# GpSimd computes nothing in the first expert slot: all low parts go to VectorE, and six weight pieces are decoded through PSUM

## The chip, the cores and the metric

One core of one Trainium2 chip runs the whole program. The metric is device time in microseconds (us). The engines are TensorE (PE; PEld is its weight load), VectorE (DVE), ScalarE (ACT), GpSimd (POOL) and SyncE (SP, which only issues DMAs here).

## The reference: what is computed

Three stages follow each other, all in float32 with 3072 tokens of width 384.

```python
# 1. linear attention with a decay: per batch, head and step t
y[t]  = r[t] @ (state + outer(u * k[t], v[t]))
state = w[t][:, None] * state + outer(k[t], v[t])
# 2. mixture of 8 experts, 384 tokens each, filled greedily by score
logits = x @ w_gate                  # tokens taken in order of their logits
out[mask_e] = relu(x[mask_e] @ w1[e]) @ w2[e]
# 3. a dense block, its weights w_in and w_out given as float64
h = x @ w_in
y = (h * clip(h + 3, 0, 6) / 6) @ w_out
```

## The kernel before

**Stages.** Attention runs first, as 24 iterations `n` (blocks of 128 tokens), in `attention`. Then `search` and `fill` find the 384 tokens of the first expert while nothing else can run on TensorE; `gather` fetches their rows by three indirect DMAs that GpSimd issues (line 958). Then come eight expert slots, `slot(p, ...)`. A slot has eight steps `f` of the expert's own layers (products `ph` and `pa`; "up part" below), and then 16 steps of the dense block (products `pg` and `py`, steps 0 to 17 with the drain; "dense part"). Search, fill and gather for expert p + 1 are cut into pieces by `yield` and run inside slot p.

**High and low parts.** Every float32 operand of a big product is split into a high part (rounded to `fp32r` by ScalarE) and a low part (value minus high part), and each product takes three of the four partial products. The low parts are `wl` (expert weights, 128x768, line 933), `hl` (hidden values, lines 995 and 998), `gl` (dense block, line 1021), `xl` (inputs, lines 969 and 1049) and the second half of `io` (dense weights, line 897).

**Decoding.** The dense block's weights come as 32 pieces of 128x384 float64, loaded into `raw`. A piece is turned into float32 by: `Abs` on ScalarE (`q`, line 862), a clamp (line 865 on GpSimd or 875 on VectorE), and three integer operations on VectorE (lines 879, 881, 883: shift, sign, lowest bits). ScalarE then makes its high part and line 897 its low part. All pieces are decoded once, and serve the eight slots. In attention 12 pieces (`EARLY`) are decoded, with the intermediate `z` in PSUM (tag `cnt`), their clamps and ten of their low parts on GpSimd. Pieces 12 to 19 are clamped by GpSimd too, at the end of attention and in the search, and one operation of line 879 stands behind each of the search's six steps (`begin`). The rest, in pairs and in SBUF (`io_stages`), is spread over slot 0: `FIRST` stages behind the gather, and then `STAGES[half]` stages in each half step.

**Order.** Nothing is scheduled by the compiler; each engine executes in the order in which the program issues. In a slot, `dve()` opens each half step: it runs what is due (`run_due`: the high and low parts of decoded pieces), then in slot 0 the decode stages, then one piece of the search if its countdown `state["wait"]` is zero. `pe()` counts down and issues the search's small matmuls. `WAITS` holds the countdowns of slot 0. `tick(t)` issues loads and the expert weights' splits.

```python
1020  nc.scalar.activation(gh, g, AF.Copy)
1021  (nc.vector if last and f >= NGT - 2 else nc.gpsimd).tensor_tensor(gl, g, gh, op=ALU.subtract)
```

These stand right behind lines 1016 (ScalarE, `r`) and 1017 (VectorE, `r`); the matmuls that read `gl(f)` are issued two steps later (`down2(f - 2)`).

Of the kernel before, what the change touches and what calls it, by code (L numbers as in the profile page):

```python
# [9 lines left out]
F32 = mybir.dt.float32  # L10
# [32 lines left out]
FIRST = 4  # L43
SATW = 2
KHDVE = (23,)
HLPOOL = (3, 6)
SPLIT0 = 22
LODVE = (0, 1)
ABSAT = 1
SPLIT = 21  # L50
QB = 8
EARLY = 12
LATER = (14, 42)
PACK = 4
STAGES = (2, 1, 0, 2, 0, 2, 3, 0, 1, 1, 2, 0, 1, 1, 3, 0, 1, 0, 0, 3, 0, 1, 0, 3, 0, 2, 0, 1, 2, 1, 1, 2, 0, 1, 1, 0, 0, 0, 0, 2, 0, 0, 0, 0, 0, 0, 0, 0)
WAITS = (2, 1, 3, 2, 2, 2, 2, 2, 2, 2, 3, 2, 2, 4, 2, 2, 2, 2, 2, 1)
# [3 lines left out]
B0 = 7  # L60
# [9 lines left out]
class Kernel:  # L70
    def __init__(self, tc, ctx, t, out):
# [7 lines left out]
        self.begun, self.q, self.raw, self.io, self.io_at = {}, {}, {}, {}, 0  # L79
# [68 lines left out]
    def attention(self):  # L148
        tc, nc, t = self.tc, self.nc, self.t
        with ExitStack() as ctx:  # L150
# [236 lines left out]
            turn = {B0 + i * 4 // 3: i for i in range(EARLY)}  # L387
            bits, his, los = iter(()), [], []

            for n in range(NU + 2):  # L390
# [6 lines left out]
                for i in range(EARLY):  # L397
                    if n == B0 + i * 4 // 3 - 3:
                        self.io_load(i)
# [236 lines left out]
    def search(self, ph, mk, es, ve):  # L636

        nc, RT, ps_r = self.nc, self.RT, self.ps_r
# [19 lines left out]
        for k, (sh, n) in enumerate(steps):  # L658
            sh2, n2 = steps[k + 1] if k + 1 < len(steps) else (0, 0)

            if ph or k:
# [33 lines left out]
            if not ph:  # L695
                self.begin(EARLY + k)
            yield SATW
            pn = ps_r.tile([128, E], F32, tag="rt", name=f"pn{ph}_{k}")
# [41 lines left out]
    def fill(self, ph):  # L740
        nc, RT, ps_r = self.nc, self.RT, self.ps_r
# [19 lines left out]
        pb = ps_r.tile([128, 2], F32, tag="rt", name=f"pb{ph}")  # L761
# [18 lines left out]
        pl = ps_r.tile([32 * pack, 24 * pack], F32, tag="rt", name=f"pl{ph}")  # L780
# [12 lines left out]
        else:  # L793
# [4 lines left out]
            times(nc.vector, OBP, NU)  # L798
        yield 3
# [10 lines left out]
        py = ps_r.tile([128, 24], F32, tag="rt", name=f"py{ph}")  # L810
# [27 lines left out]
        pc = ps_r.tile([128, E, NU], F32, tag="rt", name=f"pc{ph}")  # L838
# [29 lines left out]
    def io_bits(self, i):  # L868

        nc = self.nc  # L870
        v = self.raw[i].rearrange("p (n t) -> p n t", t=2)
        low, top, q = v[:, :, 0], v[:, :, 1], self.q[i]
        qi = q.bitcast(I32)
# [4 lines left out]
        z = self.ps_c.tile([128, DM], I32, tag="cnt", name=f"z{i}") if i < EARLY else qi  # L878
        nc.vector.tensor_scalar(z, qi, 3, 0x3FFFFFF8, op0=ALU.logical_shift_left, op1=ALU.bitwise_and)
        yield  # L880
        nc.vector.scalar_tensor_tensor(z, top, -0x40000000, z, op0=ALU.bitwise_and, op1=ALU.bitwise_or)  # L881
        yield
        nc.vector.scalar_tensor_tensor(qi, low, 29, z, op0=ALU.logical_shift_right, op1=ALU.bitwise_or)  # L883

    def begin(self, i):
        b = self.begun.setdefault(i, [self.io_bits(i), 0])
        next(b[0], None)
        b[1] += 1
# [5 lines left out]
    def io_lo(self, i):  # L894
        w = self.io[i]
        eng = self.nc.vector if i in LODVE else self.nc.gpsimd
        eng.tensor_tensor(w[:, DM:], self.q.pop(i), w[:, 0:DM], op=ALU.subtract)  # L897

    def io_stages(self):

        while self.io_at < 2 * NGT:
            j = self.io_at
            self.io_at += 2
            for k in range(3 if j in self.clamped else 4):
                some = False
                for i in (j, j + 1):
                    if i not in self.begun or self.begun[i][1] <= k:
                        self.begin(i)
                        some = True
                if k == ABSAT:  # L910
                    while j + 3 - QB in self.q:
                        self.run_due()
                    for i in (j + 2, j + 3):
                        if i not in self.clamped:
                            self.io_abs(i)
                if some:
                    yield
            self.later(1, lambda j=j: (self.io_hi(j), self.io_hi(j + 1)))
            self.later(2, lambda j=j: (self.io_lo(j), self.io_lo(j + 1)))

# [10 lines left out]
    def split(self, raw, hi, lo, eng):  # L931
        self.nc.scalar.activation(hi, raw, AF.Copy)  # L932
        eng.tensor_tensor(lo, raw, hi, op=ALU.subtract)  # L933

# [36 lines left out]
    def slot(self, p, dve, pe, tick):  # L971
# [16 lines left out]
        def up_ev(f, ph):  # L988
            hh = self.HB.tile([128, CAP], F32R, tag="hh", name=f"hh{p}_{f}", bufs=2)
            hl = self.HB.tile([128, CAP], F32R, tag="hl", name=f"hl{p}_{f}", bufs=2)  # L990
            if p == 0 and f in HLPOOL:
                h = self.HB.tile([128, CAP], F32, tag="r6", name=f"h{p}_{f}", bufs=2)
                nc.scalar.activation(h, ph, AF.Relu)
                nc.scalar.activation(hh, h, AF.Copy)
                nc.gpsimd.tensor_tensor(hl, h, hh, op=ALU.subtract)
            else:
                nc.scalar.activation(hh, ph, AF.Relu)  # L997
                nc.vector.scalar_tensor_tensor(hl, ph, 0.0, hh, op0=ALU.max, op1=ALU.subtract)  # L998
# [292 lines left out]
```

## Time and profile before

| | us |
|---|---|
| three timed runs | 899.45 (898.15 to 905.95) |
| the profiled execution | 900.43 |
| its span, first to last instruction | 898.6 |
| busy: PE, DVE, ACT, POOL | 844.7, 523.4, 426.6, 464.1 |
| first product of slot 0, of slot 1, of slot 2 | 229.53, 333.50, 414.55 |

The profile is one execution; all positions are us from the start of its span. A busy PE in attention includes matmuls on constants that fill gaps. The share of the whole span says little: PE is busy 94% of it, but the losses lie in one stretch, between the end of attention (about 193 us) and slot 1.

### The profile page before, as it was taken

The page shows a single profiled execution, that of the slowest core. Times are in us where ns is not written, and L with a number is a line of the kernel's source. Part 1 is how long each engine was busy: PE and PEld are TensorE (multiplying, and loading weights), DVE is VectorE, ACT ScalarE, POOL GpSimd, SP SyncE. Part 2 cuts the span into 40 slices and gives each one's busy share as a digit, 9 for nine tenths or more (in the row PEclk, how much of TensorE's full clock was granted, in tenths as well). Part 3 has the DMA queues.
Part 4 walks back from the last instruction along what each step waited for, and adds up shares of the span by engine and source line. Part 5 has one row for each costly group of instructions (what it writes and reads, how often), then busy time and mean ns, then how long its engine had stood idle before and what let it go on. Part 6 is the DMA issues. An engine that isn't in the chain of part 4 may idle for free.

```text
span 898.6 us, 15952 instructions
## 1 busy us (share of the span) xinstructions
PE 844.7 (94%) x5942; PEld 790.1 (88%) x5942; DVE 523.4 (58%) x1269; ACT 426.6 (47%) x1025; POOL 464.1 (52%) x428
## 2 busy tenths in 40 slices
PE   7999999964669999999999999999999999999996
PEld 4889998852568899999999999999999999999996
DVE  6879998847798765654563655355455622422211
ACT  4777777731445453444344443434444353344332
POOL 4558898744673553346337423723662383365232
PEclk7999999975779999999999999999999999999999
DMA  9997777124610050023004101300320130122000
GB/s 251 255 262 224 214 220 225 48 62 173 200 47 1 1 168 27 1 89 106 1 3 132 61 1 54 123 19 1 110 85 1 53 114 27 54 62 80 1 1 27
DMA packets 40343, 80.48 MB, mean 90 GB/s; under 512 B 4416, under 2 KB 20160, under 8 KB 40256
## 3 DMA queue, kind: packets, MB, share of 16 engines
q1 hardware_dynamic: 32576, 62.06, 23.2%
q0 software_dynamic: 3072, 9.44, 3.2%
q10 hardware_dynamic: 4608, 7.87, 2.5%
q8 instruction: 49, 0.80, 0.4%
q14 instruction: 38, 0.31, 0.1%
HBM read 69.91 MB, written 9.44 MB: 88 GB/s over the span
## 4 chain that ended last, share of the span: by engine, by line
PE 62%; DVE 7%; issue 4%; POOL 2%; ACT 1%; DMA 0%; POOLq 0%; ACTq 0%; DVEq 0%
PE pg L980 20%; PE ph L980 10%; PE py L1031 7%; PE py L1029 6%; PE py L1030 6%; PE pa L1004 3%; PE pa L1006 3%; PE pa L1005 3%; POOL gl L1021 1%; DVE q L883 1%; DVE cm L669 1%; PE cnt L679 1%; PE px L966 1%; DVE q L881 1%; POOL io L897 1%
## 5 line engine op out<-in xcount | busy, mean ns | idle before, releaser
L1021 POOL TENSOR_TENSOR gl<-r,gh 128x384 fp32r<-128x384 f32 x126 | 131.9, 1047 | 263.7 <-ACT gh L1020 263.4
L980 PE MATMUL pg<-xh,io 128*128 128x384 f32 x768 | 160.5, 344 | 0.0
L1017 DVE SCALAR_TENSOR_TENSOR r<-r,pg 128x384 f32<-128x384 f32 x128 | 70.6, 552 | 139.7 <-ACT r L1016 138.3
L933 POOL TENSOR_TENSOR wl<-we,wh 128x768 fp32r<-128x768 f32 x60 | 115.4, 1925 | 57.4 <-ACT wh L932 38.4
L980 PEld LDWEIGHTS pg<-xh,io 128*128 128x128 f32 x768 | 131.8, 188 | 2.2 <-ACT xh L1048 1.6
L1031 PE MATMUL py<-io,gl 128*128 128x384 f32 x384 | 130.7, 340 | 1.7 <-POOL gl L1021 1.6
L1029 PE MATMUL py<-io,gh 128*128 128x384 f32 x384 | 131.3, 342 | 0.0
L1030 PE MATMUL py<-io,gh 128*128 128x384 f32 x384 | 129.0, 336 | 0.0
L1016 ACT ACTIVATE r<-pg,three 128x384 f32<-128x384 f32 x128 | 74.3, 580 | 110.0 <-PE pg L980 108.3
L1020 ACT ACTIVATE gh<-r 128x384 fp32r<-128x384 f32 x128 | 67.2, 525 | 104.1 <-DVE r L1017 104.1
L980 PE MATMUL pg<-xl,io 128*128 128x384 f32 x384 | 87.6, 336 | 0.0
L1031 PEld LDWEIGHTS py<-io,gl 128*128 128x128 f32 x384 | 72.0, 188 | 5.2 <-POOL gl L1021 4.9
L998 DVE SCALAR_TENSOR_TENSOR hl<-ph,hh 128x384 fp32r<-128x384 f32 x62 | 34.4, 555 | 71.8 <-ACT hh L997 71.8
L932 ACT ACTIVATE wh<-we 128x768 fp32r<-128x768 f32 x64 | 53.6, 838 | 40.0 <-PE pa L1006 22.6
L1029 PEld LDWEIGHTS py<-io,gh 128*128 128x128 f32 x384 | 72.2, 188 | 0.2
L1030 PEld LDWEIGHTS py<-io,gh 128*128 128x128 f32 x384 | 72.2, 188 | 0.0
L980 PEld LDWEIGHTS pg<-xl,io 128*128 128x128 f32 x384 | 68.7, 188 | 0.0
L980 PE MATMUL ph<-xh,wh 128*128 128x384 f32 x192 | 67.6, 352 | 0.1
L1006 PE MATMUL pa<-hl,wh 128*128 128x384 f32 x192 | 65.4, 341 | 1.4 <-DVE hl L998 0.7
L1004 PE MATMUL pa<-hh,wh 128*128 128x384 f32 x192 | 66.3, 346 | 0.0
L980 PE MATMUL ph<-xh,wl 128*128 128x384 f32 x192 | 65.8, 343 | 0.0
L1005 PE MATMUL pa<-hh,wl 128*128 128x384 f32 x192 | 65.0, 338 | 0.0
(221 smaller groups left out, 1690.7 us busy)
## 6 DMA issues: line engine op xcount, KB each, us to landing
we<-in_w SPq DMA_DIRECT2D x64, 384.0 KB, 3.1
kr<-in_kr SPq DMA_DIRECT2D x24, 448.0 KB, 6.2
raw<-in_wio SPq DMA_DIRECT2D x24, 384.0 KB, 5.4
w<-in_wp SPq DMA_DIRECT2D x24, 226.2 KB, 6.3
v<-in_ve SPq DMA_DIRECT2D x24, 224.0 KB, 3.0
vT<-in_vT SPq DMA_DIRECT2D x24, 192.0 KB, 5.7
xd<-xt ACTq DMA_DIRECT2D x24, 192.0 KB, 4.7
raw<-in_wio ACTq DMA_DIRECT2D x8, 384.0 KB, 5.0
```

The costliest lines, as they stand in the source:

```text
L933: eng.tensor_tensor(lo, raw, hi, op=ALU.subtract)
L980: nc.tensor.matmul(ps, w[a][part], x[:, a], start=(n == 0), stop=(n == 8))
L1004: nc.tensor.matmul(pa[d], wh[:, c], hh, start=(f == 0), stop=False)
L1005: nc.tensor.matmul(pa[d], wl[:, c], hh, start=False, stop=False)
L1006: nc.tensor.matmul(pa[d], wh[:, c], hl, start=False, stop=(f == NFT - 1))
L1016: nc.scalar.activation(g, ph, AF.Relu, bias=self.three)
L1017: nc.vector.scalar_tensor_tensor(g, g, 6.0, ph, op0=ALU.min, op1=ALU.mult)
L1020: nc.scalar.activation(gh, g, AF.Copy)
L1021: (nc.vector if last and f >= NGT - 2 else nc.gpsimd).tensor_tensor(gl, g, gh, op=ALU.subtract)
L1029: nc.tensor.matmul(py[q], gh[:, c], w, start=(f == 0), stop=False)
L1030: nc.tensor.matmul(py[q], gh[:, c], v, start=False, stop=False)
L1031: nc.tensor.matmul(py[q], gl[:, c], w, start=False, stop=(f == NGT - 1))
```

## The change

- `EARLY` goes from 12 to 14: pieces 12 and 13 are decoded in attention as well, from iteration 6 on and in four of five iterations instead of three of four. `QB`, the number of `q` buffers, goes from 8 to 10.
- Pieces 14 to 19 are decoded one at a time by a new generator `io_single`, advanced by `next(self.dec)`: once or twice in each search step, once in `fill`, six times behind the gather, four times in the first steps of slot 0: 22 single operations in all. Their `z` lies in PSUM, in a bank of its own (`ps_q`); the bank comes from `ps_r`, whose small tiles now share the tag `cnt`. Only 14 and 15 are still clamped by GpSimd, the other four by VectorE.
- Pairs 20 to 31 keep the SBUF form, all four operations on VectorE.
- In slot 0 `wl`, `hl`, `gl` and the low parts of pieces 14 to 31 are made by VectorE. GpSimd keeps the indirect DMAs. Slots 1 to 7 are left as they were.
- In slot 0 the decode stages now stand behind the search's piece in each half step; `STAGES` and `WAITS` are new.

```diff
-FIRST = 4
+FIRST = 6
-HLPOOL = (3, 6)
-EARLY = 12
+EARLY = 14
+PAIRS = 20
-STAGES = (2, 1, 0, 2, 0, 2, 3, 0, 1, 1, 2, 0, 1, 1, 3, ...)
-WAITS = (2, 1, 3, 2, 2, 2, 2, 2, 2, 2, 3, 2, 2, 4, 2, 2, 2, 2, 2, 1)
+STAGES = (0, 0, 0, 0) + (1,) * 11 + (1, 0) * 17
+SINGLE = (0, 2, 2) + (0,) * 46
+WAITS = (3, 1, 2, 2, 3, 2, 3, 2, 2, 2, 2, 2, 2, 3, 2, 2, 2, 3, 2, 1)
...
@@ io_bits @@
+        pool, tag = (self.ps_c, "cnt") if i < EARLY else (getattr(self, "ps_q", None), "z")
+        z = pool.tile([128, DM], F32, tag=tag, name=f"z{i}") if i < PAIRS else q
         if i not in self.clamped:
-            nc.vector.tensor_scalar(q, q, F64LO, F64HI, op0=ALU.max, op1=ALU.min)
+            nc.vector.tensor_scalar(z, q, F64LO, F64HI, op0=ALU.max, op1=ALU.min)
             yield
...
@@ io_lo @@
-        eng = self.nc.vector if i in LODVE else self.nc.gpsimd
+        eng = self.nc.vector if i in LODVE or i >= EARLY else self.nc.gpsimd
...
+    def io_single(self):
+        for i in range(EARLY, PAIRS):
+            self.io_ahead(i, 3)
+            for _ in self.io_bits(i):
+                yield
+            self.later(1, lambda i=i: self.io_hi(i))
+            self.later(3 + (i - EARLY), lambda i=i: self.io_lo(i))
+            yield
...
@@ search, in each step k > 0 before the count, and in each step behind sat @@
+                if not ph:
+                    next(self.dec)
-                self.begin(EARLY + k)
+                next(self.dec)
...
@@ slot @@
-            if p == 0 and f in HLPOOL:
-                h = self.HB.tile([128, CAP], F32, tag="r6", name=f"h{p}_{f}", bufs=2)
...
-            (nc.vector if last and f >= NGT - 2 else nc.gpsimd).tensor_tensor(gl, g, gh, op=ALU.subtract)
+            (nc.vector if p == 0 or last and f >= NGT - 2 else nc.gpsimd).tensor_tensor(gl, g, gh, op=ALU.subtract)
...
@@ experts, behind the gather @@
-        for f in range(3):
-            self.ex_split(0, f, nc.gpsimd)
-        for _ in range(FIRST):
-            next(stages)
+        parts = [self.ex_high(0, f) for f in range(3)]
+        for _ in range(FIRST):
+            next(self.dec)
         for g in range(3):
+            self.ex_low(*parts[g], nc.vector)
             self.transposes(0, g)
-        self.ex_split(0, 3, nc.gpsimd)
+        self.ex_split(0, 3, nc.vector)
...
-                    self.ex_split(p, t + 2, nc.gpsimd)
+                    self.ex_split(p, t + 2, nc.gpsimd if p else nc.vector)
```

`ex_high` and `ex_low` are the two halves of the former `ex_split`: the ScalarE copy and the subtraction.

## Rows read from the trace of the kernel before

**Rows 1.** Stretches: length, then busy us (instructions) by engine, TensorE's granted clock, DMA

```profile
229.50:278.10 48.60, 32.79 (x178) 30.72 (x179) 45.98 (x81) 21.22 (x46) 27.96 (x20) 0.82 0.30 101
278.10:333.60 55.50, 53.38 (x331) 50.82 (x330) 42.03 (x98) 28.19 (x66) 28.79 (x28) 1.00 0.18 56
333.60:414.70 81.10, 80.74 (x508) 77.30 (x507) 43.66 (x117) 35.04 (x78) 38.05 (x31) 1.00 0.18 58
...
226.60:333.60 107.00, 88.95 (x518) 83.12 (x517) 89.12 (x179) 50.43 (x114) 59.65 (x50) 0.91 0.24 78
```

**Rows 2.** Timeline of slot 0, PE: start, us, what, [idle before, and its end]

```profile
229.53 0.44 PE L980 MATMUL ph<-xh,wh 128*128 128x384 f32 x1
...
238.99 0.32 PE L839 MATMUL pc<-nt,scale 128*128 128x192 bf16 x1 [7.62 <-DVE nt L836]
...
260.18 0.33 PE L679 MATMUL cnt<-oh,cm 128*128 128x16 bf16 x6 [5.86 <-DVE cm L669]
```

**Rows 3.** VectorE's groups by shape, 226.6 to 333.6: count, busy us, mean ns, idle before

```profile
L883 DVE SCALAR_TENSOR_TENSOR q<-raw,q 128x384 int32<-128x384 int32 x16 | 18.8, 1213 | 0.0
...
L669 DVE TENSOR_TENSOR cm<-thr,m 128x768 bf16<-128x768 f32 x6 | 5.7, 956 | 0.2
```

**Rows 4.** Tile q, then tile z, whole span: duration in ns, min/median/max

```profile
L883 DVE SCALAR_TENSOR_TENSOR q<-raw,q x20: 543/976/2200, 219.1 to 300.5; 128x384 int32<-128x384 int32 x20
...
L897 DVE TENSOR_TENSOR io<-q,io x2: 548/872/1197, 84.6 to 90.9; 128x384 fp32r<-128x384 f32 x2
...
L879 DVE TENSOR_SCALAR z<-q x12: 539/540/543, 65.8 to 168.5; 128x384 int32<-128x384 int32 x12
```

**Rows 5.** GpSimd's groups by shape in slot 0

```profile
L897 POOL TENSOR_TENSOR io<-q,io 128x384 fp32r<-128x384 f32 x20 | 22.1, 1129 | 1.0 <-ACT io L892 1.0
L1021 POOL TENSOR_TENSOR gl<-r,gh 128x384 fp32r<-128x384 f32 x16 | 17.4, 1093 | 29.2 <-ACT gh L1020 29.1
L933 POOL TENSOR_TENSOR wl<-we,wh 128x768 fp32r<-128x768 f32 x8 | 15.4, 1938 | 10.9 <-issue 10.5 <-ACT wh L932 0.4
```

**Rows 6.** Timeline of the first gather, 218 to 227

```profile
218.11 0.18 DVE L816 TENSOR_REDUCE idx<-ly 128x3 int32<-128x24 f32 x1
...
220.69 2.40 POOL L958 DMA_INDIRECT xg<-xd,idx  x1 [4.00 <-DVE q L881]
221.01 1.02 DVE L883 SCALAR_TENSOR_TENSOR q<-raw,q 128x384 int32<-128x384 int32 x2
223.40 0.95 POOL L958 DMA_INDIRECT xg<-xd,idx  x1 [0.30 <-issue]
...
226.67 0.56 DVE L969 SCALAR_TENSOR_TENSOR xl<-px,xh 128x384 fp32r<-128x384 f32 x1 [4.64 <-ACT xh L968]
```

**Rows 7.** Timeline of the first search, steps 1 and 2

```profile
199.63 1.17 DVE L669 TENSOR_TENSOR cm<-thr,m 128x256 bf16<-128x256 f32 x4
...
202.27 1.50 POOL L865 TENSOR_SCALAR q<-q 128x384 f32<-128x384 f32 x1 [0.56 <-ACT q L862]
202.33 1.46 DVE L669 TENSOR_TENSOR cm<-thr,m 128x256 bf16<-128x256 f32 x4
...
204.21 0.34 DVE L879 TENSOR_SCALAR q<-q 128x384 int32<-128x384 int32 x1
```

**Rows 8.** VectorE's groups by shape in slot 1, 333.4 to 414.7

```profile
L669 DVE TENSOR_TENSOR cm<-thr,m 128x768 bf16<-128x768 f32 x6 | 8.7, 1468 | 0.2
```

**Rows 9.** Timeline of slot 0, dense part: VectorE, ScalarE and GpSimd

```profile
279.61 0.55 DVE L1017 SCALAR_TENSOR_TENSOR r<-r,pg 128x384 f32<-128x384 f32 x1
...
280.19 0.53 ACT L1020 ACTIVATE gh<-r 128x384 fp32r<-128x384 f32 x1 [0.86 <-DVE r L1017]
...
280.80 1.18 POOL L1021 TENSOR_TENSOR gl<-r,gh 128x384 fp32r<-128x384 f32 x1 [9.30 <-ACT gh L1020]
...
286.53 0.61 DVE L875 TENSOR_SCALAR q<-q 128x384 f32<-128x384 f32 x2
...
324.47 0.96 DVE L933 TENSOR_TENSOR wl<-we,wh 128x768 fp32r<-128x768 f32 x1 [1.33 <-ACT wh L932]
...
333.04 0.54 DVE L969 SCALAR_TENSOR_TENSOR xl<-px,xh 128x384 fp32r<-128x384 f32 x1
```

**Rows 10.** Two iterations of attention: stretches as in the first group

```profile
109.30:116.60 7.30, 7.30 (x79) 6.57 (x78) 6.94 (x20) 5.56 (x17) 7.22 (x9) 1.00 0.87 257
116.60:123.90 7.30, 7.30 (x79) 6.57 (x78) 5.93 (x12) 6.00 (x18) 5.25 (x5) 1.00 0.72 212
```

More of the change, by code (lines that the diff above doesn't have):

```diff
@@ L386, in attention @@
             counted = []
[L387 removed]
+            turn = {B0 + i * 5 // 4: i for i in range(EARLY)}
             bits, his, los = iter(()), [], []
@@ L760, in fill @@
         yield "expert"
-        pb = ps_r.tile([128, 2], F32, tag="rt", name=f"pb{ph}")
+        pb = ps_r.tile([128, 2], F32, tag="cnt", name=f"pb{ph}")
         a, b = s[:, NU - 1:NU], s[:, 2 * NU - 1:2 * NU]
@@ L779, in fill @@
         oa = RT.tile([128, NU, 24], F16, tag="oa", name=f"oa{ph}", bufs=1)
-        pl = ps_r.tile([32 * pack, 24 * pack], F32, tag="rt", name=f"pl{ph}")
+        pl = ps_r.tile([32 * pack, 24 * pack], F32, tag="cnt", name=f"pl{ph}")
         i0 = self.digits[0]
@@ L809, in fill @@
         yield 1
-        py = ps_r.tile([128, 24], F32, tag="rt", name=f"py{ph}")
+        py = ps_r.tile([128, 24], F32, tag="cnt", name=f"py{ph}")
         nc.tensor.matmul(py, self.spread[0:32 * pack], lx, start=True, stop=True)
@@ L895, in io_lo, with io_ahead @@
         w = self.io[i]
-        eng = self.nc.vector if i in LODVE else self.nc.gpsimd
+        eng = self.nc.vector if i in LODVE or i >= EARLY else self.nc.gpsimd
         eng.tensor_tensor(w[:, DM:], self.q.pop(i), w[:, 0:DM], op=ALU.subtract)
-    def io_stages(self):
[L901 to L916, printed above, removed]
+    def io_ahead(self, i, n):
+        for m in range(i, min(i + n, 2 * NGT)):
+            if m not in self.q:
+                while m - QB in self.q:
+                    self.run_due()
+                self.io_abs(m)
+    def io_single(self):
[6 more added lines that the diff above has]
+            yield
+    def io_stages(self):
+        for j in range(PAIRS, 2 * NGT, 2):
+            self.io_ahead(j, 4)
+            a, b = self.io_bits(j), self.io_bits(j + 1)
+            for k in range(4):
+                next(a, None)
+                next(b, None)
+                if k < 3:
                     yield
@@ L1101, in experts @@
         self.io_next = KEPT + AHEAD
-        self.io_at = EARLY
-        late = list(range(KEPT, EARLY + QB))
+        self.dec = self.io_single()
         pw = self.ps_a.tile([128, 512], F32, tag="a", name="pw_")
@@ L1138, in decode @@
             def decode():
+                for _ in range(SINGLE[state["half"]]):
+                    next(self.dec, None)
                 for _ in range(STAGES[state["half"]]):
@@ L1146, in dve @@
                     return
-                later = p == 0 and state["half"] in LATER
-                if p == 0 and not later:
-                    decode()
                 if state["wait"] == 0:
```

65 lines of the change are left out of this document (27 added, 38 removed).

## The prediction, made before the changed kernel ran

> **What bounds the kernel now.** I looked first for the stretch that could give time back. Slots 1 to 5 repeat one another, so slot 1 is the measure of what TensorE needs: 81.1 us, of which it is busy 80.7 [rows 1]. Slot 0 does the same products, but its first one starts at 229.53 [rows 2] and slot 1 follows at 333.6: 104 us. So the first slot holds 23 us that are not TensorE's own work, and the stretch table tells where: in the up part and shortly behind it (229.5 to 278.1) TensorE is busy 32.8 of 48.6 us and VectorE 46.0; in the dense part TensorE is back at 53.4 of 55.5 and VectorE still at 42.0 [rows 1]. TensorE's two longest idles end on VectorE's results for the search, 7.62 us before `pc` and 5.86 us before a count [rows 2]; both small matmuls stand in TensorE's order ahead of products that were ready. VectorE, then, sets the pace of slot 0's first half, and over the whole slot it works 89.1 of 107 us [rows 1].
>
> Part of that work is waiting that looks like work. The last decode operation (line 883) takes 543 to 2200 ns on the same shape [rows 4], on average 1213 in slot 0 [rows 3], while an operation of the same size that writes `z` in PSUM takes 539 to 543 with GpSimd busy beside it [rows 4]. GpSimd's own subtractions stretch too: 1129 ns for `io`, 1093 for `gl` [rows 5]. Sixteen operations of line 883 alone hold 18.8 us where 16 x 0.55 = 8.8 would do. So the question is whether VectorE, freed of GpSimd's company, can also carry GpSimd's work.
>
> **The change, part by part.** The sum is made against the profiled execution, 900.43 us (its span is 898.6); the median of the runs, 899.45, lies 1 us below.
>
> *Attention.* Two more pieces: three VectorE operations each, about 1.6 us, and on GpSimd a clamp and a low part. An iteration lasts 7.30 us with decode work or without, and TensorE is busy in all of it; VectorE has 6.94 with and 5.93 without, GpSimd 7.22 and 5.25 [rows 10]. The two pieces go to iterations that have the room, so I take 0. If that cover were gone the cost is 2 x 1.6 = 3.2 us; a gain is excluded, since TensorE has no idle there to give. GpSimd has two clamps less at the end of attention; nothing of the search waits for them, so 0.
>
> *Search.* Six short operations (0.34 us, line 879 [rows 7]; 0.27 from one start to the next, from two in 0.61 [rows 9]) become PSUM ones at about 0.47 from start to start: 6 x 0.2 = 1.2 us, on the path, because the next reduction stands behind them. Five more, 0.47 each, stand between the threshold and `sat`, while TensorE counts. They cost between 0 and 2.4 us; VectorE has little idle there, so I take 1.6. Gone are the GpSimd clamps beside three of the comparisons: 1.46 us with one, 1.17 without [rows 7], so 3 x 0.3 = 0.9 less. Net +2.0, between 0 and 2.7. The one in `fill` runs while TensorE multiplies: 0.
>
> *Gather.* The index list is done at 218.29, but the first descriptor generation ends at 223.09, and the next ones take 0.95 [rows 6]. VectorE's decode stages run in between, the last from 221.01 on, two operations in 1.02, so until 222.03 [rows 6]; 222.03 + 0.95 is 222.98, 0.1 short of the end seen. I read it as GpSimd standing still until VectorE's stages are over. The new operations there have one input or both in PSUM. Then the first generation runs 0.3 behind the list: 218.29 + 2.0 + 0.3 + 0.95 = 221.54 instead of 223.09, and everything behind is 1.6 us earlier. The Trainium skill speaks against this reading (SBUF — State Buffer, "Who interferes with whom"): an operation of two tensors takes only the read side of the port pair that VectorE shares with GpSimd, and descriptor generation, it infers, needs the write side. By it the first generation is slow by itself and the whole would end 3.6 us later; that is a rival below.
>
> *VectorE's stream through slot 0*, from the first `xl` (226.67 before [rows 6], now 225.1) to the last `xl` of the next gather (ends 333.58 [rows 9]), without GpSimd beside it. From start to start a two-input operation on 384 columns takes 0.47 (two of them 1.02, of 0.55 each [rows 6]), one on 768 columns 0.87 (0.96 [rows 9] less the same overlap), a clamp or shift 0.27.
> - Search, list and bookkeeping: slot 1's 43.7 us [rows 1], less 31 operations of `hl`, `r` and `xl` at 0.55 (17.1), less the stretch of its six comparisons, 8.7 [rows 8] against 5.7 [rows 3]: 23.6.
> - `r` and now `gl`, 16 each: `gl` follows right behind `r` in VectorE's order, and has to wait for ScalarE's `gh` in between. From `r` to the start of `gl` it is 280.80 - 279.61 = 1.19, of which about 0.64 is VectorE standing idle [rows 9]. 16 x (1.19 + 0.47) = 26.6. Queued behind each such wait are the decode stages and the search; who waits for those is TensorE's next count.
> - `hl` 8 and `xl` 9: 17 x 0.47 = 8.0. `wl` 11 (seven of them GpSimd's before): 9.6. Low parts of pieces 14 to 31, 18 x 0.47 = 8.5.
> - Six pairs, two times (0.27 + 0.27 + 0.47 + 0.47) each: 17.8. The four single operations: 2.0.
>
> Together 96.1 us. Add waits: the four late `wl` still stand right behind ScalarE's `wh` (1.33 us idle each before [rows 9]; about 0.4, since `gl` now fills the time in between) and the first `r` of the dense part: 2.2. So the stream ends at 225.1 + 98.3 = 323.4 instead of 333.58: **10.2 us earlier**. TensorE needs 81 from about 228, so it is not the bound.
>
> Inside the slot the gain is uneven. The up part holds `hl` and `xl` 5.2, four `wl` 3.5, ten low parts 4.7, the single operations 2.0, 11 of the 24 pair stages 8.2 and about 10 of the search: 33.6 us where 48.6 were spent. Some 4 us lie ahead of it, so the dense part keeps 98.3 - 33.6 - 4 = 60.7 where 55.5 were: of 15 us won early, 5 are given back. What is late next is `gl`: TensorE's `down2` of two steps before.
>
> Low parts taken off GpSimd free no one else: it sat idle 29 us waiting for `gh` [rows 5]. The shared `cnt` tag puts a count behind the readers of the tile before it, which the search's own order does already: 0, at most 1 us. Slots 1 to 7 stay.
>
> The sum: 900.4 - 10.2 = 890.2. Its bounds: no waits, a free search and the 1 us of the median give 885 (2.2 + 2.0 + 1.0 less), and 884 with start-to-start times that I rounded up; all of VectorE's former idle kept (107 - 89.1 = 17.9 against 2.2) gives 906. I take the low end, because TensorE is ahead of VectorE in this plan and its results wait for VectorE, not the other way round; but not all of it.
>
> **The rivals.**
> - *TensorE is the bound after all* (VectorE's work overlaps better than start to start): slot 0 takes 81 us from 228, slot 1 starts at 309, so 876. Against it stands a sum of 96 us on one engine; for it nothing but errors of mine. 0.08.
> - *The gather is not freed*: +3.6, 894. For it the skill's rule, against it the 0.1 us fit above. 0.12.
> - *TensorE's clock.* In the up part VectorE leaves TensorE some 1.5 us idle in every step. Before, the granted clock averaged 0.82 in that stretch [rows 1]. At half clock a step's 18 matmuls take 18 x 0.33 = 5.9 us against VectorE's 4.3; four such steps cost 6.4: 896 to 897. 0.13.
> - *GpSimd is not what stretches VectorE* (the change doesn't bring what it says): 12 operations of line 883 stay 0.67 longer (8.0), 18 low parts 0.32 (872 against 548 ns [rows 4], 5.8): 904. The constant 540 ns beside a busy GpSimd speaks against it. 0.03.
> - *Slower than before: the lead is lost.* If TensorE in the dense part has no lead over VectorE, each step becomes one chain: product (1.57), `r` on ScalarE (0.6), `r`, `gh`, `gl`; VectorE then idles 2.2 us more in that step. It eats the gain from five of the 16 steps on (10.2 / 2.2); at ten it gives 890 + 22 = 912. For it: TensorE's counts stand in order ahead of the products, as in the 5.86 us case. Against: `gl` has two steps of slack, and VectorE is the later engine. 0.06.
>
> **How the numbers follow.** The forecast, VectorE's stream as the bound with few waits, has 0.58 and its own range 885 to 896. The range 884 to 901 takes in the gather, the clock and two thirds of the idle kept (890 + 10.5); outside are TensorE as the bound, the stretch that stays and the lost lead: 0.17. This kernel can't tell a change under 1% from none: faster is below 890.5, slower above 908.4. The forecast lies at that line, a little more than half of its 0.58 below it (0.32); with TensorE as the bound and small shares of the others faster has 0.43, slower 0.08 (the lost lead and part of the stretch and the kept idle), the rest, 0.49, is within 1%.
>
> **What would show it.** Line 883 on `q` at 0.55 us throughout; three generations of the first gather in a row, 0.95 each, some 0.3 behind the list; the search about 2 us longer; slot 0's first product near 228, the end of the up part near 263, slot 1 near 323; VectorE busy over 85% of slot 0, with about 0.6 us before each `gl`. The prediction is wrong if `gl` or the counts leave VectorE idle for more than 10 us, if the clock stays low in the up part, or if slots 1 to 7 change length.

## The result, and the profile after

The changed kernel takes 891.17 us (median of 20 runs, 888.75 to 912.57), the kernel before 900.17 in the same session (20 runs, 897.05 to 921.53); the ratio is 0.9911, with a 95% interval of 0.9882 to 0.994. The forecast was 890 (890.2 by the prediction's sum). The profiled execution took 902.12: it lost some 11 us at the start of attention, which the change doesn't touch and where TensorE's granted clock was 0.53 from 10 to 50 us (0.83 before). So positions are counted here from the first matmul of the search (`pn`, at 197.96 before and 208.83 after), and stretches are compared, not totals. By that count the attention takes no time more or less: in the profile of gl_deferred below, which has 0.83 there, `pn` starts at 198.02. The times given for each kernel below are those of its runs without such a loss, while the ratios take in some runs that lost about 10 us, which widens their intervals.

| us | before | after | forecast |
|---|---|---|---|
| search, first `pn` to the index list | 20.33 | 20.98 (repeat: 20.55) | +2.0 |
| first `pn` to slot 0's first product | 31.57 | 30.03 | 30 |
| slot 0, up part | 48.6 | 35.3 | 33.6 |
| slot 0, dense part | 55.4 | 60.4 | 60.7 |
| VectorE's stream, first `xl` to last `xl` | 106.9 | 99.2 | 98.3 |
| slot 1 to the end | 565.13 | 565.78 | unchanged |

The gain is 1.5 us ahead of slot 0 and 8.3 in it (103.97 to 95.70); 0.65 go again in slots 1 to 7: 9.2 in all, against 10.2.

The stretches that answer to [rows 1]: the up part, the dense part, slot 1, VectorE's stream (columns as there):

```profile
238.90:274.20 35.30, 31.00 (x177) 28.05 (x178) 33.52 (x84) 17.15 (x37) 0.00 (x0) 0.95 0.35 126
274.20:334.60 60.40, 55.11 (x332) 52.18 (x331) 48.06 (x130) 29.11 (x69) 3.73 (x4) 0.97 0.18 57
334.60:415.50 80.90, 80.56 (x507) 77.14 (x506) 43.22 (x116) 34.99 (x78) 38.01 (x31) 1.00 0.17 54
235.10:334.30 99.20, 87.80 (x515) 80.91 (x516) 84.13 (x216) 47.03 (x108) 3.62 (x3) 0.97 0.26 88
```

VectorE (the third of the busy times) is busy 33.5 of 35.3 us in the up part, TensorE (the first) 31.0: VectorE is the bound there. In the dense part TensorE is busy 55.1 of 60.4 and VectorE 48.1; neither is full. GpSimd's 28 us of the up part are gone, and the granted clock there is 0.95 instead of 0.82.

VectorE's groups by shape, slot 0 (answering [rows 3], [rows 4] and [rows 5]; line 886 was 883, 895 was 897, 953 was 933, 1027 was 1021):

```profile
L895 DVE TENSOR_TENSOR io<-q,io 128x384 fp32r<-128x384 f32 x18 | 9.4, 549 | 0.0
L1027 DVE TENSOR_TENSOR gl<-r,gh 128x384 fp32r<-128x384 f32 x16 | 8.9, 559 | 9.5 <-ACT gh L1026 9.5
L953 DVE TENSOR_TENSOR wl<-we,wh 128x768 fp32r<-128x768 f32 x9 | 8.6, 952 | 0.9 <-ACT wh L948 0.9
...
L886 DVE SCALAR_TENSOR_TENSOR q<-raw,q 128x384 int32<-128x384 int32 x12 | 6.1, 546 | 0.0
...
L879 DVE TENSOR_SCALAR q<-q 128x384 f32<-128x384 f32 x12 | 3.7, 350 | 0.0
```

Line 886 takes 546 ns on the mean where it took 1213, though it still works in SBUF: the stretch is gone with the company. Ahead of each of the 16 `gl` VectorE stands idle for 0.59 us, until ScalarE's `gh` is ready.

TensorE's timeline, answering [rows 2]: the first product, `pc`, and the longest idle left in the up part:

```profile
238.86 0.44 PE L992 MATMUL ph<-xh,wh 128*128 128x384 f32 x1
...
242.11 0.26 PE L841 MATMUL pc<-nt,scale 128*128 128x192 bf16 x1
...
255.85 0.45 PE L1012 MATMUL pa<-hl,wh 128*128 128x384 f32 x1 [1.79 <-DVE hl L1004]
```

`pc` had waited 7.62 us; now it comes without idle time, and what TensorE waits for in the up part is `hl`, 1.79 us at most.

The first gather, answering [rows 6]:

```profile
229.63 0.18 DVE L818 TENSOR_REDUCE idx<-ly 128x3 int32<-128x24 f32 x1
...
230.76 1.19 POOL L970 DMA_INDIRECT xg<-xd,idx  x1 [2.48 <-DVE z L884]
...
232.26 0.96 POOL L970 DMA_INDIRECT xg<-xd,idx  x1 [0.31 <-issue]
...
233.23 0.95 DVE L953 TENSOR_TENSOR wl<-we,wh 128x768 fp32r<-128x768 f32 x1
233.52 1.49 POOL L970 DMA_INDIRECT xg<-xd,idx  x1 [0.30 <-issue]
```

The first generation ends 2.14 us behind the list (4.80 before), the third 5.20 behind it (7.32 before). The third takes 1.49, with a `wl` beside it.

A step of the search, answering [rows 7]: from one `mx` to the next, with a comparison and two decode operations of a single piece between:

```profile
215.68 0.16 DVE L712 TENSOR_REDUCE mx<-pn 128x1 int32<-128x8 f32 x1
...
216.09 1.16 DVE L668 TENSOR_TENSOR cm<-thr,m 128x256 bf16<-128x256 f32 x4
...
217.47 0.55 DVE L886 SCALAR_TENSOR_TENSOR q<-raw,z 128x384 int32<-128x384 int32 x1
217.93 0.15 DVE L695 TENSOR_TENSOR sat<-cnt,rem 32x8 bf16<-32x8 f32 x1
218.13 0.56 DVE L879 TENSOR_SCALAR z<-q 128x384 f32<-128x384 f32 x1
...
218.60 0.15 DVE L712 TENSOR_REDUCE mx<-pn 128x1 int32<-128x8 f32 x1
```

It is 2.92 us long here; the same step was 2.59 to 2.63. `cm` is back at 1.16 (1.46 with GpSimd's clamp). An iteration of attention that answers to the first of [rows 10]:

```profile
120.17:127.47 7.30, 7.30 (x81) 6.55 (x80) 6.96 (x19) 5.88 (x18) 7.14 (x8) 1.00 0.84 239
```

### The profile page after: what moved, and what is told of

Its sections match the earlier page's. It is cut to its first block, busy times and chain, and to the rows that moved or that the text cites. A ratio compares the mean times of both kernels' runs of the same rounds, so it can differ in the third digit from the quotient of the medians.

```text
span 900.3 us, 15960 instructions
## 1 busy us (share of the span) xinstructions
PE 854.7 (95%) x5942; PEld 797.3 (89%) x5942; DVE 525.5 (58%) x1317; ACT 424.9 (47%) x1023; POOL 403.9 (45%) x380
## 4 chain that ended last, share of the span: by engine, by line
PE 59%; DVE 10%; issue 3%; ACT 3%; POOL 1%; DMA 0%; POOLq 0%; DVEq 0%; ACTq 0%
PE pg L992 20%; PE ph L992 10%; PE py L1037 6%; PE py L1035 6%; PE py L1036 6%; PE pa L1010 3%; PE pa L1012 3%; PE pa L1011 3%; DVE cm L668 1%; DVE r L1023 1%; ACT gh L1026 1%; DVE wl L953 1%; ACT wh L948 1%; DVE io L895 1%; PE px L978 1%
## 5 line engine op out<-in xcount | busy, mean ns | idle before, releaser
L1027 POOL TENSOR_TENSOR gl<-r,gh 128x384 fp32r<-128x384 f32 x110 | 115.3, 1048 | 234.1 <-ACT gh L1026 234.0
L953 POOL TENSOR_TENSOR wl<-we,wh 128x768 fp32r<-128x768 f32 x52 | 100.2, 1926 | 46.0 <-ACT wh L948 37.8
L970 POOL DMA_INDIRECT xg<-xd,idx x24 | 24.6, 1027 | 98.7 <-DVE idx L818 90.4
```

Of the source, the lines that this page charges most:

```text
L953: eng.tensor_tensor(l, raw, h, op=ALU.subtract)
L1027: (nc.vector if p == 0 or last and f >= NGT - 2 else nc.gpsimd).tensor_tensor(gl, g, gh, op=ALU.subtract)
```

## The experiments

**The changed kernel once more** (no edit).

> The changed kernel once more, for a profile whose TensorE clock is full in attention. Every theory: 889 to 892 us. If VectorE's stream is the bound, from the first xl to the last xl of the next gather it lasts 98 to 99 us with 9 to 10 us of idle in front of the 16 gl, and nothing else idle for more than 4 us.

Measured: 889.4 to 891.6 us, ratio 0.9909 (0.9837 to 0.9982). Slot 0 took 95.67, the stream 99.27, first `pn` to first product 29.95. The stretches repeat to 0.1 us, so a difference of 0.5 in them means something; the search, at 20.55, repeats less well.

### Does GpSimd's company stretch VectorE, and what is it worth?

**gpsimd_company**: a useless GpSimd subtraction in each half step of slot 0.

```diff
+        idle = [M.tile([128, DM], F32, name=f"idle{i}") for i in range(3)]
+        for i in range(2):
+            nc.gpsimd.memset(idle[i], 1.0)
...
+                if p == 0 and not skip:
+                    nc.gpsimd.tensor_tensor(idle[2], idle[0], idle[1], op=ALU.subtract)
```

> The changed kernel with one useless GpSimd subtraction (128x384, two inputs in SBUF, nothing waits for it) in each of the 47 half steps of slot 0, about 1 us each. Theory (company stretches VectorE's two-input SBUF operations): line 886 on q goes from 0.55 us to 0.7 or more, the stream grows by about 0.5 x 47 = 23 us: 905 to 915. Rival (the stretch before had another cause): 891, durations unchanged.

Measured: 918.0 to 920.1 us, ratio 1.0163 (1.0056 to 1.0269), above the 905 to 915 of the theory. Up and dense part, and three of VectorE's groups in slot 0:

```profile
229.40:290.00 60.60, 38.87 (x178) 35.90 (x178) 58.81 (x84) 17.44 (x37) 45.71 (x39) 0.77 0.21 75
290.00:350.40 60.40, 54.01 (x331) 50.56 (x330) 49.37 (x130) 29.02 (x69) 8.23 (x7) 1.00 0.17 52
```

```profile
L895 DVE TENSOR_TENSOR io<-q,io 128x384 fp32r<-128x384 f32 x18 | 14.6, 840 | 0.0
...
L879 DVE TENSOR_SCALAR q<-q 128x384 f32<-128x384 f32 x12 | 6.9, 619 | 0.0
...
L1004 DVE SCALAR_TENSOR_TENSOR hl<-ph,hh 128x384 fp32r<-128x384 f32 x8 | 4.4, 548 | 0.0
```

The same work keeps VectorE busy 108.2 us instead of 81.6: 26.6 more, for 50.2 us of GpSimd work that nobody waits for (53.9 against 3.7), or 0.53 us for each us of it. Most of the company fell in the up part, which became 25 us longer, nearly all of it VectorE's. The granted clock there fell to 0.77 and TensorE is busy 38.9 us instead of 31.0, but it still stands idle 21.7. The stretch is not the same for all operations: `io`, with two inputs in SBUF, goes from 549 to 840 ns and the clamp, with one, from 350 to 619, while `hl`, with one input in SBUF and one in PSUM, stays at 548 (547 in the changed kernel).

**low_on_gpsimd**: one half of the change undone. `wl`, `gl` and the low parts of pieces 14 to 31 are GpSimd's again in slot 0; PSUM pieces, order and countdowns stay.

```diff
-        eng = self.nc.vector if i in LODVE or i >= EARLY else self.nc.gpsimd
+        eng = self.nc.vector if i in LODVE else self.nc.gpsimd
...
-            (nc.vector if p == 0 or last and f >= NGT - 2 else nc.gpsimd).tensor_tensor(gl, g, gh, op=ALU.subtract)
+            (nc.vector if last and f >= NGT - 2 else nc.gpsimd).tensor_tensor(gl, g, gh, op=ALU.subtract)
...
-            self.ex_low(*parts[g], nc.vector)
+            self.ex_low(*parts[g], nc.gpsimd)
...
-        self.ex_split(0, 3, nc.vector)
+        self.ex_split(0, 3, nc.gpsimd)
...
-                    self.ex_split(p, t + 2, nc.gpsimd if p else nc.vector)
+                    self.ex_split(p, t + 2, nc.gpsimd)
```

> One half of the change undone: in slot 0 the low parts of the expert weights (wl), of the dense block (gl) and of the decoded pieces 14 to 31 are GpSimd's again (42 subtractions); the pieces in PSUM, the order and the countdowns stay as in the changed kernel. Theory: GpSimd's company costs VectorE about as much as the work is worth to it. VectorE is rid of 16 gl and 18 io at 0.47 and of 8 wl at 0.87, 23 us, and pays 0.41 to 0.57 us for each of 42 GpSimd subtractions (prices of gl_on_gpsimd and gpsimd_company), 17 to 24 us: VectorE's busy time in the stream stays within 78 to 86 us (84.1 now), slot 0 at 92 to 98 (95.7 now), the time at 887 to 893. Then the gain of the whole change came from its other half. Rival, the prediction's reading: work taken off GpSimd is the gain, and slot 0 goes back toward 104, the time to 897 to 900.

Measured: 900.9 to 902.4 us, ratio 1.0026 (1.0004 to 1.0048); slot 0 108.3. The theory of that moment, which I had formed from gl_on_gpsimd (below), falls; the prediction's reading stands. Up and dense part, VectorE's decode groups of one input, and the two largest waits of TensorE:

```profile
226.70:270.40 43.70, 32.20 (x177) 29.72 (x178) 40.18 (x69) 17.39 (x37) 22.80 (x17) 0.92 0.33 115
270.40:335.00 64.60, 56.21 (x332) 53.30 (x331) 45.83 (x106) 29.02 (x69) 28.94 (x28) 0.95 0.15 53
```

```profile
L879 DVE TENSOR_SCALAR q<-q 128x384 f32<-128x384 f32 x12 | 8.6, 753 | 0.0
L882 DVE TENSOR_SCALAR q<-q 128x384 int32<-128x384 int32 x12 | 7.7, 684 | 0.0
```

```profile
PE pa L1012 <- DVE hl L1004: 8.9, 5, 3.6
PE pg L992 <- POOL io L895: 5.4, 1, 5.4
```

VectorE has 23.1 us less to do (16 `gl` 8.9, 18 `io` 9.4, five of the nine `wl` 4.8) and is busy 86.0 instead of 81.6: company costs 27.5 us for 48.0 us of GpSimd work (51.7 less 3.7), 0.57 per us, near the price in gpsimd_company. The clamp of a pair takes 753 ns where it took 350. So in the changed kernel VectorE does GpSimd's work and its own in less time (81.6) than its own work takes beside GpSimd's (86.0). That is not all of the 12.6 us of slot 0. The up part is 8.4 longer here, with VectorE busy 6.7 more; in the dense part VectorE is busy 2.2 less, and the 4.2 by which it is longer stand beside TensorE's 5.4 of waiting for an `io` from GpSimd, which needs 1.08 us for each. This kernel keeps the new order, countdowns and PSUM pieces of the change and is no faster than the kernel before, so these alone bring nothing; whether the moved low parts would bring their gain in the old order no run shows.

**gl_on_gpsimd**: only `gl` goes back to GpSimd.

```diff
-            (nc.vector if p == 0 or last and f >= NGT - 2 else nc.gpsimd).tensor_tensor(gl, g, gh, op=ALU.subtract)
+            (nc.vector if last and f >= NGT - 2 else nc.gpsimd).tensor_tensor(gl, g, gh, op=ALU.subtract)
```

> Only gl of slot 0 goes back to GpSimd. Theory (VectorE's stream is the bound, GpSimd's company stretches it): the stream loses 16 x (0.59 + 0.47) = 17 us and gets back 16 subtractions as company at 0.5 us each (23 us over 46 GpSimd operations before), so 9 us less: about 882. Rival (the company costs more than gl and its wait, over 1.06 us each): 891 or more. Rival (TensorE or the shift of pieces into attention is what counts): 891, no change.

Measured: 886.3 to 889.2 us, ratio 0.9817 (0.9714 to 0.992), not the 882 of the theory; slot 0 93.6. The dense part:

```profile
275.00:332.90 57.90, 53.77 (x332) 50.53 (x331) 45.52 (x114) 29.13 (x69) 21.90 (x20) 1.00 0.18 59
```

For `gl` alone the trade goes the other way. It takes 18.4 us off VectorE (8.9 of work, 9.5 of waiting for `gh`) and costs 6.5 in company (VectorE is busy 79.2 in slot 0, and would be at 81.6 - 8.9 = 72.7 without), 0.36 us for each of GpSimd's 18.2. Of the difference only 2.1 reach the end; TensorE's own work fills 53.8 of the 57.9 us.

### What are gl's waits worth, and what is late next?

**gl_deferred**: `gl` stays on VectorE, but is issued one half step later, when `gh` is ready.

```diff
-            (nc.vector if p == 0 or last and f >= NGT - 2 else nc.gpsimd).tensor_tensor(gl, g, gh, op=ALU.subtract)
+            if p == 0:
+                self.later(0 if f == NGT - 1 else 1, lambda: nc.vector.tensor_tensor(gl, g, gh, op=ALU.subtract))
+            else:
+                (nc.vector if last and f >= NGT - 2 else nc.gpsimd).tensor_tensor(gl, g, gh, op=ALU.subtract)
```

> gl stays on VectorE, but is issued half a step later, behind the next piece of search and decode, so that VectorE need not stand idle until ScalarE's gh is done. Theory: the 16 waits of 0.59 us go, 9 us less: 881 to 883. Rival (VectorE isn't the bound, TensorE's order or its clock is): 891, no change. Rival (a later gl makes TensorE's second product wait): above 891.

Measured: 889.6 and 889.7 us, ratio 0.99 (0.974 to 1.0059), not the 881 to 883 of the theory, and by itself not to be told from no change; the stretches show one, with slot 0 at 93.7. Its two parts, and VectorE's waits (us in total, times, longest):

```profile
228.10:263.80 35.70, 32.05 (x177) 29.60 (x178) 33.63 (x84) 17.38 (x37) 0.00 (x0) 0.90 0.36 126
263.80:321.90 58.10, 54.27 (x332) 50.48 (x331) 46.62 (x130) 28.98 (x69) 3.02 (x4) 1.00 0.18 55
```

```profile
DVE wl L953 <- ACT wh L948: 5.7, 6, 1.3
DVE sm L692 <- ACT lo L684: 3.6, 3, 1.2
```

The 9.5 us before `gl` are gone, but VectorE now waits elsewhere (`wl` 5.7 instead of 0.9, and for the counts): its idle time in the slot only falls from 14.1 to 13.5, and the slot is 2.0 shorter. The dense part needs 54.3 of TensorE's own in any case, so it had no more than 6.1 of its 60.4 to give.

**gl_deferred_stages_later**: gl_deferred, and six decode stages go from the up part, where VectorE is full, to the dense part.

```diff
-STAGES = (0, 0, 0, 0) + (1,) * 11 + (1, 0) * 17
+STAGES = (0, 0, 0, 0) + (1, 0) * 5 + (1,) * 19 + (0,) * 16
```

> The gl_deferred kernel with six decode stages moved out of the up part of slot 0 into the dense part, and the rest of the pairs done by half step 32 (STAGES alone is changed). Theory: with gl off VectorE's waiting path, the up part is still bound by VectorE (busy 33.6 of 35.7 us in gl_deferred) while the dense part is bound by TensorE (54.3 busy of 58.0). Six stages of about 0.75 us taken out of the up part make it 31 to 32 us; the dense part, where VectorE has room, stays at 56 to 58. Slot 0 (93.7 in gl_deferred) comes to 88 to 90, the median of undisturbed runs to 884 to 886. Rival: what the up part gains the dense part gives back, since VectorE still has the same work to do between the first xl and the last: slot 0 stays at 93 to 94, 889 to 890. Second rival: the late weights arrive late for TensorE's pg, dense part above 60.

Measured: 885.3 to 887.8 us, ratio 0.9795 (0.966 to 0.9929).

```profile
248.90:280.40 31.50, 29.17 (x177) 26.59 (x178) 28.73 (x72) 15.59 (x33) 0.00 (x0) 1.00 0.40 139
280.40:341.00 60.60, 54.28 (x331) 50.60 (x330) 51.77 (x143) 30.67 (x73) 3.25 (x4) 1.00 0.18 56
```

The up part gained 4.2 us, as expected; the dense part gave 2.5 back, so slot 0 came to 92.1, between the theory (88 to 90) and the rival (93 to 94).

**list_early**: the changed kernel, with two countdowns of the search at 2 instead of 3.

```diff
-WAITS = (3, 1, 2, 2, 3, 2, 3, 2, 2, 2, 2, 2, 2, 3, 2, 2, 2, 3, 2, 1)
+WAITS = (3, 1, 2, 2, 3, 2, 3, 2, 2, 2, 2, 2, 2, 2, 2, 2, 2, 2, 2, 1)
```

> The changed kernel with the countdowns ahead of two late steps of the search in slot 0 at 2 instead of 3, so that the next expert's index list is made one half step of two earlier and its rows arrive earlier. Theory: VectorE's own stream sets the end of slot 0, and of the end only the 1.2 us in which slot 1's third group of products waits for its rows can be won: the dense part goes from 60.4 to 59.2 at best, time 890 to 891. Rival: the chain list, gather, rows is what ends the slot, and the slot shortens by a step's share: dense part 57 to 57.5, 888. If the counts come too early for their inputs, VectorE and TensorE wait for each other and the slot gets longer, 892 to 895.

Measured: 888.1 to 889.2 us, ratio 0.9818 (0.9685 to 0.9952); slot 0 94.7, the dense part 59.4. The time is that of the rival, but the slot that of the theory: the list came 3.0 us earlier in the slot (83.3 us behind its first product, 86.3 in the changed kernel), and the slot ended only 1.0 earlier, so the list doesn't set its end. What is won is the wait of 1.3 us that TensorE had for the third rows.

**all_three**: the three edits together.

> The changed kernel with the three edits that each shortened slot 0 together: gl issued one half step later, six decode stages moved from the up part to the dense part, the index list one step earlier. If they add up, slot 0 is 95.7 - 2.0 - 1.6 - 1.0 = 91.1 us and the median of undisturbed runs 884 to 885. Rival: the list, coming earlier, meets the six moved stages on VectorE in the dense part, and the earlier list gives nothing: slot 0 92, 886 as gl_deferred_stages_later. TensorE's own 81 us is the floor and isn't reached.

Measured: 885.6 to 886.1 us, ratio 0.9839 (0.9741 to 0.9937).

```profile
227.50:259.00 31.50, 29.18 (x177) 26.60 (x178) 28.73 (x72) 15.48 (x33) 0.00 (x0) 1.00 0.40 143
259.00:318.20 59.20, 54.11 (x331) 50.67 (x330) 51.23 (x142) 31.07 (x73) 3.25 (x4) 1.00 0.17 55
```

Slot 0 is 90.7; the three add up in it, and the kernel is some 5 us below the changed one. TensorE is busy 83.3 of the 90.7.

### What held the first gather?

**gather_decode_sbuf**: `z` of pieces 17 to 19, decoded behind the list, in SBUF.

```diff
-        z = pool.tile([128, DM], F32, tag=tag, name=f"z{i}") if i < PAIRS else q
+        z = pool.tile([128, DM], F32, tag=tag, name=f"z{i}") if i < PAIRS - 3 else q
```

> The changed kernel with the intermediate z of the last three single pieces (17 to 19), decoded while the first gather's descriptors are made, in SBUF instead of PSUM; all else the same. Theory of the prediction: VectorE operations with both inputs in SBUF hold up GpSimd's descriptor generation, so the first generation, which ends 2.14 us behind the list in the changed kernel, ends 3.4 us or more behind it, the first product of slot 0 comes 1.3 us later. Rival: generation isn't held up by such operations and the first one is slow by itself: 2.1 to 2.2 us behind the list as now, and the first product at the same distance from the list.

Measured: 891.6 us (one run). The first generation ends 2.15 behind the list, as with PSUM, not the 3.4 or more of the theory. That says little of the mechanism: the two operations of two SBUF inputs that come ahead of it were over 1.05 us behind the list, and it starts 0.95 behind it in any case. But the second took 1.31 instead of 0.96, with such operations beside it:

```profile
220.98 0.56 DVE L886 SCALAR_TENSOR_TENSOR q<-raw,q 128x384 int32<-128x384 int32 x1
221.06 1.31 POOL L970 DMA_INDIRECT xg<-xd,idx  x1 [0.30 <-issue]
221.46 0.95 DVE L953 TENSOR_TENSOR wl<-we,wh 128x768 fp32r<-128x768 f32 x1
```

**gather_no_decode**: nothing of VectorE's beside the gather; six decode steps and the three `wl` come later.

```diff
-FIRST = 6
+FIRST = 0
...
-SINGLE = (0, 2, 2) + (0,) * 46
+SINGLE = (2, 4, 4) + (0,) * 46
...
+            self.transposes(0, g)
             self.ex_low(*parts[g], nc.vector)
-            self.transposes(0, g)
             warm(REWARM[1])
```

> The changed kernel with no decoding and no low part of the expert's weights on VectorE while the first gather's three descriptor generations run: the six stages go to the first three half steps of slot 0, each wl behind its group's transposes. Theory of the prediction: with nothing beside it the first generation starts 0.3 us behind the list and the three take 0.95 each, so the third ends 3.2 us behind the list (5.19 in the changed kernel). Rival: the first generation of a program is late and long by itself (0.95 us behind the list, 1.19 long) whatever VectorE does, and only the third loses the 0.5 us by which a wl lengthens it: 4.5 to 4.7 us behind the list. Slot 0's up part gets the six stages and so 2 to 3 us longer.

Measured: the rival, and 917.3 us (one run, its `pn` at 219.12).

```profile
239.78 0.18 DVE L818 TENSOR_REDUCE idx<-ly 128x3 int32<-128x24 f32 x1
240.91 1.19 POOL L970 DMA_INDIRECT xg<-xd,idx  x1 [2.47 <-ACT wh L948]
242.41 0.96 POOL L970 DMA_INDIRECT xg<-xd,idx  x1 [0.30 <-issue]
243.67 0.94 POOL L970 DMA_INDIRECT xg<-xd,idx  x1 [0.30 <-issue]
```

With nothing beside it the first generation still starts 0.95 behind the list and takes 1.19; the third ends 4.65 behind the list instead of 5.20. Slot 0 was 101.6 (up part 40.9, 5.6 longer and not 2 to 3), so the work moved costs more there than the gather gives.

**gather_eight_ops**: gather_no_decode with eight useless operations of two SBUF inputs, back to back behind the list. Two memsets of GpSimd in the setup fill their inputs.

```diff
+        idle = [M.tile([128, DM], I32, name=f"idle{i}") for i in range(4)]
+        for i in range(2):
+            nc.gpsimd.memset(idle[i], 1)
...
+        for i in range(8):
+            nc.vector.scalar_tensor_tensor(idle[2 + i % 2], idle[0], 29, idle[1], op0=ALU.logical_shift_right, op1=ALU.bitwise_or)
```

> The gather_no_decode kernel with eight useless VectorE operations of two SBUF inputs (128x384, int32, two outputs in turn, none waiting for another, as the eight decode operations that stand behind the list in the kernel before) right behind the index list. Theory: such operations back to back hold up descriptor generation: the first generation, which ends 2.14 us behind the list in gather_no_decode, ends about 1.0 us behind the last of the eight, that is 4.6 to 5.0 us behind the list, as in the kernel before (4.81). Rival: before, something else held it up (the landing of rows, the clamps on GpSimd), and here it ends 2.1 to 2.5 us behind the list. In either case the two generations behind it are 0.95 each.

Measured: 898.1 us (one run).

```profile
218.38 0.18 DVE L818 TENSOR_REDUCE idx<-ly 128x3 int32<-128x24 f32 x1
218.47 3.83 DVE L1130 SCALAR_TENSOR_TENSOR idle<-idle,idle 128x384 int32<-128x384 int32 x8
221.95 1.41 POOL L970 DMA_INDIRECT xg<-xd,idx  x1 [4.93 <-DVE idle L1130]
223.66 0.96 POOL L970 DMA_INDIRECT xg<-xd,idx  x1 [0.30 <-issue]
```

The first generation ends 4.80 behind the list and 1.06 behind the last of the eight operations (222.30), as in the kernel before: 4.80 and 1.07 (222.03 [rows 6]). First `pn` to first product is 31.62, before 31.57. But that does not show that the eight operations held it. In gpsimd_company the operations of VectorE behind the list are those of the changed kernel, and the first generation starts nearly as late:

```profile
217.44 0.18 DVE L818 TENSOR_REDUCE idx<-ly 128x3 int32<-128x24 f32 x1
220.85 1.18 POOL L970 DMA_INDIRECT xg<-xd,idx  x1 [4.75 <-DVE z L884]
224.55 5.63 POOL L1153 TENSOR_TENSOR idle<-idle,idle 128x384 f32<-128x384 f32 x4
```

It starts 3.23 behind the list, before any of the useless subtractions. What gpsimd_company shares with gather_eight_ops, and with no other run, are two more memsets of GpSimd in the setup. In these two and in the kernel before, the trace has a fetch of instructions by DMA (queue q14) between the list and the start of the first generation; in gpsimd_company, from 217.62 to 220.85:

```profile
q14 instruction: 1, 0.01, 0.9%
```

It begins 1.10, 1.23 and 0.25 us behind the list, and the generation starts 2.13, 2.17 and 2.16 behind that beginning, with VectorE's operations back to back or without them. In the eleven runs in which the generation starts 0.95 behind the list, no fetch of this queue begins there until 2.2 behind it. So the start goes with that fetch and not with VectorE's operations; whether the fetch is its cause no run tests. The length does go with VectorE's operations. It is 1.18 to 1.19 in the eleven runs and in gpsimd_company, 1.41 here, where the eight ran beside the generation for 0.35 us, and 2.40 in the kernel before, where they ran beside it for 1.34.

**singles_sbuf**: `z` of all six single pieces in SBUF.

```diff
-        z = pool.tile([128, DM], F32, tag=tag, name=f"z{i}") if i < PAIRS else q
+        z = pool.tile([128, DM], F32, tag=tag, name=f"z{i}") if i < EARLY else q
```

> The other half undone: the intermediate z of the six single pieces 14 to 19 lies in SBUF as before the change, everything else as in the changed kernel. Prediction's sizes: PSUM makes each clamp and shift 0.2 us longer, and five of them stand on the search's path, so the search gets about 1.2 us shorter (20.98 us from its first pn to the index list now, then 19.8); the first descriptor generation is held up. Theory now: the operations lie beside TensorE's counts, and the search stays at 20.5 to 21.0; the second generation is 0.35 longer as in gather_decode_sbuf, the third not; slot 0 unchanged at 95 to 96.5; time 889 to 892, no difference that can be measured. If PSUM for six pieces were what brought the gain, slot 0 would be 98 or more.

Measured: 888.0 to 890.4 us, ratio 0.9878 (0.9774 to 0.9981): not to be told from the changed kernel. The search took 20.13, first `pn` to first product 29.24, slot 0 95.67. PSUM for these six pieces brings nothing; it costs the search 0.4 to 0.9 us.

## Why the prediction was right

**What bounds the kernel** held: VectorE's stream through slot 0 sets its first half. It went from 106.9 to 99.2 us; the forecast was 98.3. The cause was tested from both sides: useless GpSimd work on the changed kernel makes slot 0 25 us longer, and giving GpSimd its subtractions back makes it 108. Both give about half a us of VectorE's time for each us of GpSimd's work (0.53 and 0.57; with `gl` alone it is 0.36). A rule of the Trainium skill (SBUF — State Buffer, "Who interferes with whom") says that a VectorE operation with two SBUF inputs contends with a GpSimd instruction that reads SBUF. The trace of gpsimd_company agrees with it for `io` (549 to 840 ns) beside an unchanged `hl` (548); the stretch of the clamp, which has one input (350 to 619), it doesn't cover. How it is shared in one pair of operations (line 886 kept 548 ns in low_on_gpsimd while the clamp went to 753) no run here shows.

**Attention** at nothing: right.

**Search** at +2.0: mis-sized. It came out at 0.2 and 0.65 more in the changed kernel's two profiles (20.57 to 21.28 in the ten variants that keep its search, so up to 0.95). In the step shown the terms are near what was taken: `sat` stands 0.34 further behind `cm` (0.32 taken of the 0.47), the `mx` behind it 0.27 further (0.2), `cm` is 0.3 shorter (0.3). Most of the miss lies in what the prediction did not look at: 0.43 us that VectorE stood idle in the first step are gone, and from the last `mx` to the list it takes 6.10 us instead of 6.58; the other 0.4 is spread over the steps.

**Gather**: the net of search and gather, 1.6 earlier, came to 1.5 at the first product, by two errors that cancel. "The first generation runs 0.3 behind the list", and 0.95 long, was wrong: the first one is 0.95 behind and 1.19 long with VectorE idle (gather_no_decode), so it ends 0.9 later than forecast; the pace was that of the generations behind it. The third took 0.54 more with a `wl` beside it. The search's missing 1.35 paid for both. The mechanism, GpSimd standing still until VectorE's stages are over, holds for a part only. The first generation ended 4.80 behind the list before and 2.14 now. Of these 2.66 us, 1.21 are its length (2.40 to 1.19), which goes with VectorE's operations beside it, and 1.45 its start (2.40 to 0.95), which goes with the instruction fetch (gather_eight_ops beside gpsimd_company). Nothing in the prediction foresaw the second part, so it is luck that the gain ahead of slot 0 came out as forecast; why the fetch moved stays open. Single operations lengthened later generations by 0.35 (1.31 instead of 0.96) and 0.54 (1.49). The rival drawn from the Trainium skill (the same section of SBUF — State Buffer), by which descriptor generation isn't held by operations of two tensors, fails against these lengths: the third generation takes 1.49 with a `wl` beside it and 0.94 without (gather_no_decode); the measurement decides. PSUM was not what helped: in singles_sbuf, with `z` in SBUF, the first generation starts and lasts as in the changed kernel.

**VectorE's stream**: 96.1 us, with 16 waits of 0.64 for `gh` in it, plus 2.2. Measured: 84.1 busy and 15.0 idle, with 0.59 before each `gl` (9.5 together), 5.6 elsewhere. So the work was 1.8 less than the sum (96.1 - 10.2 = 85.9) and the waits 2.7 more. Not foreseen was how little the waits are worth: gl_deferred removes the 9.5 us and wins 2.0, as VectorE waits elsewhere instead and TensorE's own 54 us stand behind it in the dense part.

**Up and dense part**: 33.6 and 60.7 against 35.3 and 60.4. The up part is bound by VectorE, as said; its 1.7 more are idle time (1.8) of VectorE there. The dense part gave 5.0 back of the 13.3 won before it, the 5 of the prediction.

**The rivals.** TensorE as the bound did not come, and in the dense part it is near. The clock stayed at 0.95 in the up part. The lead was not lost: TensorE never waits for `gl` in slot 0 of the changed kernel. GpSimd is what stretches VectorE (gpsimd_company).

**Slots 1 to 7** are 0.65 longer, some 0.1 each (0.3 to 1.1 in the variants); why stays open, as does how a generation shares its time with a single operation.

## What to carry to other kernels

Price an operation on a second engine by what it costs the first: here a us of GpSimd's subtractions cost VectorE about half a us, in all more than they took there (27.5 against 23.1 us). The one whose input comes late (`gl`) was as well left where it was (slot 0 93.6) or issued later (93.7). A wait counted on one engine is worth only what the next bound leaves of it, so look for the floor of the other engine in that stretch before claiming it. When a sum comes out right, test its terms: here errors of 0.9 + 0.54 and 1.35 us cancelled. And look for what else a test changes: two memsets in the setup go with a gather 2.3 us later.

## What I had not expected of the hardware

- In eleven of the 14 traces the first descriptor generation of the first gather starts 0.95 us behind its list and takes 1.18 to 1.19, with nothing of VectorE's beside it too (gather_no_decode). In the second gather it starts 0.27 behind it, and takes 0.96 to 1.03.
- In the other three (before, gpsimd_company, gather_eight_ops) it starts 2.40 to 3.40 us behind the list, each time 2.1 to 2.2 behind the beginning of an instruction fetch, whatever VectorE does.
- A descriptor generation takes 0.94 to 0.96 us by itself and 1.49 with one VectorE subtraction of two SBUF inputs, 768 columns wide, beside it.
- Beside GpSimd's subtractions in low_on_gpsimd, VectorE's clamp and shift with one SBUF input stretched more (350 to 753, 348 to 684 ns) than the last operation, with two (546 to 548); in gpsimd_company that one went to 680.
